# Block-sparse attention with a feed-forward layer: the first six tiles' scores as one product per block, neighbouring keys copied beside the sampled ones

## The chip, the cores and the metric

The kernel runs on one core of a Trainium2 chip. TensorE (PE in the profile), VectorE (DVE), ScalarE (ACT) and GpSimd (POOL) each work through their own instruction stream in order; SyncE (SP) issues most of the transfers, POOL and ACT some. The metric is the device time of one execution in microseconds, lower is better. Before the change three runs gave 733.46, 733.47 and 734.31 us, a median of 733.47 us.

## The reference

Four batches of 768 tokens, 8 heads of 64 numbers, blocks of 32 tokens (24 blocks per batch). The attention is masked by blocks, and its output goes through a feed-forward layer with a squared ReLU:

```python
scores = scale * np.matmul(q, k.transpose(0, 1, 3, 2))
mask = np.abs(blk_i - blk_j) <= window            # window = 1: the neighbouring blocks
mask = mask | (blk_i == 0) | (blk_j == 0) | (blk_i == n_blocks - 1) | (blk_j == n_blocks - 1)
mask[qb's rows, kb's columns] = True              # three sampled blocks per query block
attn = softmax(where(mask, scores, -1e9));  x = attn @ v
h = np.maximum(x @ w_in, 0.0)                     # 3072 x 512 by 512 x 2048
return h * h @ w_out                              # 3072 x 2048 by 2048 x 512
```

So a query block (other than the first and the last) sees 8 blocks of keys: two fixed ones (first and last), three sampled, three neighbouring. The first and the last query block see everything. All is float32.

## The kernel before

**Tiles.** A tile is 128 tokens of a batch, four query blocks; a batch has six tiles, and three tiles make a chunk, the unit of the feed-forward layer. There are 24 tiles and 8 chunks. A `Half` is one tile with four of the eight heads; a `Whole` is the first and the last query block of a batch with one pair of heads. Below, H10 is the half of tile 1 with heads 0 to 3, H11 that with heads 4 to 7, and W0 to W3 are the four wholes of batch 0.

**Stages.** The head (to about 50 us) does W0, W1, H00, W2, W3, H01, H10, H11, H20, H21 in this order, five steps of a hand-written clock (`now`) apart. Then comes chunk 0 of the feed-forward layer, and beside it the halves of tiles 3 to 5; later chunks run beside later tiles. A half goes through fixed steps: scores (PE, into PSUM), maxima (DVE), exponentials (ACT), turn (PE transposes into PSUM), copies (out of PSUM into `pT`, one of 512 numbers per partition for each of `e` = 0 and 1), values (PE, line 532), norm (DVE, lines 548 to 563). The classes yield how many steps of the clock to wait; within an engine the instructions run in the order in which this loop emits them, so an instruction that waits holds up all behind it on its engine.

**Keys.** `KN` holds all keys of the batch, by block. `KG` holds per query block up to 8 slots: two fixed, three sampled, three neighbouring. From tile 6 on (`MOVED`) the slots are loaded by DMA (`load_kg`), and the scores are one product of 256 columns per block and head (line 408). For the first six tiles POOL copies fixed (line 308) and sampled blocks (line 278) from `KN` into `KG`, and the scores take two products: 96 columns of neighbours straight from `KN` and 160 columns from `KG` (both line 426).

**Values.** `V[k][0]` has the two fixed blocks and two sampled ones for each query block of tile k, `V[k][1]` the third sampled one and three neighbours. Sampled blocks come by DMA on SP (`load_sampled`, line 334), nine or twelve transfers per tile. The fixed ones of tile 0's first query block come by DMA and are copied by ACT to the other places (`copy_static`, line 218). Neighbours of tile 0 come by DMA (`load_window`, line 320); those of tiles 1 and 2 are copied from `vn`, all values of the batch (`copy_window`, line 226): 36 copies on POOL, 12 on ACT.

**Weights.** `cut_load` (POOL, line 801) fetches a raw block, `cut` (ACT, lines 817 and 819) and `cut_bits` (DVE, lines 828 and 829) turn it into float32. In chunk 0 each block is then split into two parts by ACT (line 861) and POOL (line 864; lines 835 and 836 for the first one).

Of the kernel before, what the change touches and what calls it, by code (L numbers as in the profile page):

```python
# [10 lines left out]
F32 = mybir.dt.float32  # L11
# [11 lines left out]
B, H, S, D = 4, 8, 768, 64  # L23
BLK = 32
NBLK = S // BLK
NRAND = 3
P = 128
NT = S // P
NJ = P // BLK
NPAIR = H // 2  # L30
# [44 lines left out]
CUT_0 = (35, 5)  # L75
CUT_1 = 3

MOVES_0 = 22


FIXED_0 = 7
FIRST_LOADS, SECOND_LOADS, THIRD_LOADS = 2, 3, 4
LATE = (0, 4)
KEYS_N = 2
MOVED = 6
# [1 line left out]


WO_LOW = 3
PLAIN = 16  # L90


# [5 lines left out]
def tile_block_sparse_attention_moe(ctx: ExitStack, tc, kd, knd, qd, qgd, vd, vnd, samp, wcat, out):  # L98
# [60 lines left out]
    QG = one.tile([P, NPAIR, 2, BLK], F32, name="QG")  # L159
    KN = one.tile([P, 2, NBLK, 2, BLK], F32, name="KN")  # L160
    V = {0: [one.tile([P, NJ, 2, HW // 2], F32, name=f"V{c}") for c in range(2)]}
    W1 = {f: one.tile([P, DM], F32, name=f"W1{f}") for f in range(1, NF)}
    KG = [one.tile([P, NJ, NSLOT // BLK, NPAIR, BLK], F32, name=f"KG{i}") for i in range(2)]
    WO = {f: one.tile([P, DM], F32, name=f"WO{f}") for f in range(WO_LOW)}

# [68 lines left out]
    def groups(t):  # L234

        return (2, 3, 1) if t == 0 else tuple(range(NJ - 1 if t == NT - 1 else NJ))

    def centre(qb):
        return min(max(qb, 1), NBLK - 2)
# [12 lines left out]
    def load_q(b, t, eng=nc.sync, own=None):  # L252
        q = (own or rot).tile([P, NJ, NPAIR, BLK], F32, tag="q", name=f"q{b}_{t}", bufs=1 if own else 2)
        n = NJ * NPAIR * BLK
        eng.dma_start(q.rearrange("p a b c -> p (a b c)"), qd[b, :, t * n : (t + 1) * n])
        st["q", b, t] = q

    def keys_of(b, t, own):

        k = order.index((b, t))  # L260
        st["kg", b, t] = (
            own.tile([P, NJ, 2 + NRAND, NPAIR, BLK], F32, name=f"KG{k}") if own else KG[(k - (k >= UC)) % 2]
        )
        return st["kg", b, t]

    def copy_keys(b, t, own=None):

        vals = sampled(t, 0, POOL)
        kg = keys_of(b, t, own)
        for us in (slice(0, 1), slice(1, 2)) if t == 0 else (slice(0, 2),):  # L270
            if t < UC:
                for u in range(us.start, us.stop):
                    static_keys(b, t, u, nc.gpsimd.tensor_copy)
            for j in sorted(groups(t)):
                for r in range(NRAND):
                    to = kg[:, j, 2 + r].rearrange("p (u i) s -> p u (i s)", u=2)
                    of = KN.rearrange("p u k i s -> p u k (i s)")
                    nc.gpsimd.tensor_copy(to[:, us].unsqueeze(2), of[:, us, bass.ds(vals[NRAND * j + r], 1)])  # L278
                yield
# [3 lines left out]

    def load_kg(b, t):
        vals = sampled(t, 0, SP)
        kg = keys_of(b, t, None)
        k4 = kd[b].rearrange("p (a c) -> p a c", a=NBLK)
        for j in sorted(groups(t)):
            for r in range(NRAND):
                nc.sync.dma_start(  # L290
                    kg[:, j, 2 + r].rearrange("p b c -> p (b c)").unsqueeze(1), k4[:, bass.ds(vals[NRAND * j + r], 1), :]
                )
        if t < 2:
            for i in range(2):
                src = k4[:, i * (NBLK - 1)].unsqueeze(1)
                dst = kg[:, :, i].rearrange("p j b c -> p j (b c)")
                nc.sync.dma_start(dst, src.broadcast_to(list(dst.shape)))
        js = sorted(groups(t))
        src = k4[:, NJ * t + js[0] - 1]
        n = src.shape[-1]  # L300
        src = bass.AP(src.tensor, src.offset, [src.ap[0], [n, len(js)], [1, 3 * n]])
        nc.sync.dma_start(kg[:, js[0] : js[0] + len(js), 2 + NRAND :].rearrange("p j w b c -> p j (w b c)"), src)

    def static_keys(b, t, u, copy):

        src = st["kn", b, u][:, 0 : NBLK : NBLK - 1].rearrange("p i a c -> p i (a c)").unsqueeze(1)
        dst = st["kg", b, t][:, :, 0:2, 2 * u : 2 * u + 2].rearrange("p j i a c -> p j i (a c)")
        copy(dst, src.broadcast_to(list(dst.shape)))

    def load_window(k, u, eng=nc.sync):  # L310
        us = halves(k, u)
# [48 lines left out]
    class Half:  # L360
# [37 lines left out]

        def scores(self):
            b, t, u = self.b, self.t, self.u  # L400
            q, kg, kn = st["q", b, t], st["kg", b, t], st["kn", b, u]
            self.sb = [bank(f"s{self.name}_{e}") for e in range(2)]
            for i in range(2) if self.moved else ():
                pr = 2 * u + i
                for g, j in enumerate(self.js):
                    for e in range(2):
                        r = slice(e * D, (e + 1) * D)
                        nc.tensor.matmul(  # L408
                            self.sb[e][g * BLK : (g + 1) * BLK, i * NSLOT : (i + 1) * NSLOT],
                            q[r, j, pr, :],  # L410
                            kg[r, j, :, pr, :],
                            start=True,
                            stop=True,
                        )
            for i in range(2) if not self.moved else ():
                pr = 2 * u + i
                for piece in range(2):
                    for g, j in enumerate(self.js):
                        c = centre(NJ * t + j)
                        for e in range(2):  # L420
                            r = slice(e * D, (e + 1) * D)
                            if piece == 0:
                                k, a, z = kn[r, c - 1 : c + 2, i, :], S_WIN, NSLOT
                            else:
                                k, a, z = kg[r, j, : 2 + NRAND, pr, :], 0, S_WIN
                            nc.tensor.matmul(  # L426
                                self.sb[e][g * BLK : (g + 1) * BLK, i * NSLOT + a : i * NSLOT + z],
                                q[r, j, pr, :],
                                k,
                                start=True,  # L430
                                stop=True,
                            )

        def maxima(self):
            m = self.m = rot.tile([P, 2, 2], F32, tag="m", name=f"m{self.name}", bufs=4)
# [59 lines left out]
        def copies(self, pt):  # L495
            self.pT = rot.tile([P, NJ, 4, 2, BLK], F32, tag="pT", name=f"pT{self.name}", bufs=2)
            n = len(self.js)
            for e in range(2):
                src = pt[e].rearrange("p (h j q) -> p h j q", h=4, j=NJ)[:, :, :n]
                dst = self.pT[:, :n, 2 * e : 2 * e + 2].rearrange("p j i c q -> p (i c) j q")  # L500
                if e == 0 or self.k < UC:
                    nc.scalar.copy(dst, src)
                else:
                    nc.vector.tensor_copy(dst, src)
# [340 lines left out]
    def cut_next():  # L845

        nonlocal done
        n = len(cuts)
        for stage, lag in ((cut, AHEAD), (cut_bits, AHEAD + 1), (cut_split, AHEAD + 2), (cut_load, 0)):
            if 0 <= done - lag < n:  # L850
                stage(*cuts[done - lag])
        done += 1
# [150 lines left out]
    for k in range(1, UC):  # L1003
# [4 lines left out]
    load_keys(0, 1, nc.gpsimd)  # L1008
    load_sampled(0, 0, nc.sync, SP)
    load_q(0, 1)  # L1010
    load_sampled(1, 0, nc.sync, SP)
    load_q(0, 2, own=begin)
    load_sampled(2, 1, nc.sync, SP)
    windows = {
        (k, u): [(copy_window, k, u, j, n) for j in range(NJ) for n in range(3)]
        for k in range(1, UC)
        for u in range(2)
    }
    first = copy_keys(0, 0)
    for _ in groups(0):  # L1020
        next(first)
# [3 lines left out]
    for _ in range(EARLY_CUTS):  # L1025
        cut_next()
    deque(copy_keys(0, 1), 0)
    for i in range(AHEAD + 1):
        if i == FIRST_LOADS:
            for f, *at in windows[1, 0]:  # L1030
                f(*at, nc.gpsimd.tensor_copy)
        if i == SECOND_LOADS:
            deque(copy_keys(0, 2, begin), 0)
        if i == THIRD_LOADS:
            for f, *at in windows[2, 0] + windows[2, 1]:
                f(*at, nc.gpsimd.tensor_copy)
        if EARLY_CUTS <= i < AHEAD:
            cut_next()
    fixed = [(copy_static, k, i) for k in range(UC) for i in range(2)]
    moves = windows[1, 1]  # L1040
    side = lambda name: ps_o.tile([P, 512], F32, tag="o", name=name)
    work = Stream()
    for at, u in units(0):
# [2 lines left out]
    while work.todo or work.running:  # L1046
        work.step(now)
        now += 1
        if now % KEYS_N == 0 and later and next(later[0], True):
            later.pop(0)  # L1050
        if now >= FIXED_0 and fixed:
            f, *at = fixed.pop(0)
            f(*at, nc.scalar.copy)
        if now >= MOVES_0 and moves:
            f, *at = moves.pop(0)
            f(*at, nc.scalar.copy)
        if now >= CUT_0[0] and (now - CUT_0[0]) % CUT_0[1] == 0:
            cut_next()
    start.__exit__(None, None, None)
# [85 lines left out]
```

## Time and profile before

| | |
|---|---|
| median of the runs | 733.47 us |
| time of the profiled execution | 733.34 us |
| its span, first to last instruction | 731.6 us |
| PE busy | 707.5 us (97%) |
| DVE, ACT, POOL busy | 513.6, 507.2, 502.5 us (69 to 70%) |
| granted TensorE clock | 0.999 |
| moved by DMA | 108.42 MB |

In a row of the timeline the columns are the start in us, the duration, engine, source line, operation, output and input tiles with their shapes, the count, and in brackets the idle time of the engine ahead of it and what ended it. Rows of the groups give count, busy us and mean ns of one, then the idle time ahead of them. SPq and ACTq are instructions that issue transfers. PE is at 97% over the whole span, but at 5, 7 and 8 tenths in the first slices of 18.3 us: the head is where PE has room.

### The profile page before, as it was taken

How to read it: one execution, taken by the hardware profiler on the slowest of the kernel's cores; microseconds unless marked ns; L12 is line 12 of the kernel's file. 1: busy time of each engine (PE TensorE's matmuls, PEld its weight loads, DVE VectorE, ACT ScalarE, POOL GpSimd, SP SyncE). 2: the span in 40 equal slices, each digit the busy share in tenths (PEclk: the TensorE clock that was granted, in tenths of full speed). 3: DMA queues.
4: the chain of work that ended last, by engine and by line, in shares of the span. 5: the costliest groups of instructions: out<-in, count | busy, mean ns of one | idle time of the engine just before them, and what ended most of it. 6: DMA issues, size and time to landing. Idle time of an engine off the chain costs nothing.

```text
span 731.6 us, 22308 instructions
## 1 busy us (share of the span) xinstructions
PE 707.5 (97%) x8000; PEld 577.6 (79%) x8000; DVE 513.6 (70%) x1018; ACT 507.2 (69%) x1122; POOL 502.5 (69%) x606
## 2 busy tenths in 40 slices
PE   5789999999999999999999999999999999999997
PEld 3676775677888888877888888887888888889896
DVE  5876665868787867668886876768887676645442
ACT  5977777988876875588877776578877777533222
POOL 5994444347876676768878577666877577768884
PEclk9999999999999999999999999999999999999999
DMA  9958899746445547656455457665555351101001
GB/s 278 271 144 262 248 272 337 207 114 202 130 112 141 167 99 221 190 126 176 125 131 145 126 146 218 173 144 173 134 138 146 97 164 45 35 1 44 1 1 43
DMA packets 99232, 108.42 MB, mean 148 GB/s; under 512 B 13985, under 2 KB 85666, under 8 KB 99122
## 3 DMA queue, kind: packets, MB, share of 16 engines
q1 hardware_dynamic: 92866, 83.42, 42.7%
q0 software_dynamic: 5680, 22.27, 9.3%
q8 instruction: 64, 1.05, 0.6%
q10 hardware_dynamic: 576, 1.31, 0.5%
q14 instruction: 46, 0.38, 0.2%
HBM read 100.65 MB, written 6.29 MB: 146 GB/s over the span
## 4 chain that ended last, share of the span: by engine, by line
PE 80%; ACT 6%; DVE 5%; POOL 4%; issue 2%; DMA 1%; POOLq 1%; ACTq 0%; DVEq 0%
PE ph L901 34%; PE po L941 32%; PE s L408 5%; PE pv L517 5%; POOL V L226 2%; PE po L930 2%; POOL KG L278 2%; PE pv L702 1%; ACT craw L819 1%; DMA V<-in_v_dram 1%; PE g L636 1%; ACT p L477 1%; DVE WO L828 1%; DVE WO L829 1%; ACT wi L861 1%
## 5 line engine op out<-in xcount | busy, mean ns | idle before, releaser
L463 ACT ACTIVATE pm<-p 32x256 f32<-32x256 f32 x528 | 219.3, 415 | 24.6 <-DVE p L446 16.6
L864 POOL TENSOR_TENSOR wi<-W,wi 128x512 fp32r<-128x512 f32 x120 | 156.3, 1303 | 69.0 <-ACT wi L861 30.1
L901 PE MATMUL ph<-xh,wi 128*128 128x384 f32 x960 | 201.1, 347 | 2.0 <-DVE wi L863 1.6
L901 PEld LDWEIGHTS ph<-xh,wi 128*128 128x128 f32 x960 | 170.2, 188 | 25.8 <-issue 11.0
L864 POOL TENSOR_TENSOR wo<-WO,wo 128x512 fp32r<-128x512 f32 x112 | 145.1, 1295 | 51.7 <-DVE wo L863 50.9
L941 PE MATMUL po<-wo,gh 128*128 128x512 f32 x672 | 175.3, 396 | 0.0
L905 ACT ACTIVATE r<-ph 128x384 f32<-128x384 f32 x128 | 62.7, 490 | 151.3 <-PE ph L901 150.9
L920 POOL TENSOR_TENSOR gl<-gf,gh 128x384 fp32r<-128x384 f32 x112 | 113.8, 1016 | 71.9 <-DVE gf L917 59.6
L917 DVE SCALAR_TENSOR_TENSOR gf<-ph,r 128x384 f32<-128x384 f32 x112 | 61.9, 552 | 124.0 <-ACT r L905 124.0
L941 PEld LDWEIGHTS po<-wo,gh 128*128 128x128 f32 x672 | 124.0, 188 | 25.9 <-issue 4.5
L901 PE MATMUL ph<-xl,wi 128*128 128x384 f32 x480 | 103.9, 338 | 0.0
L941 PE MATMUL po<-wo,gl 128*128 128x512 f32 x336 | 98.6, 402 | 0.0
L901 PEld LDWEIGHTS ph<-xl,wi 128*128 128x128 f32 x480 | 85.4, 188 | 0.1
L941 PEld LDWEIGHTS po<-wo,gl 128*128 128x128 f32 x336 | 62.1, 189 | 21.5 <-issue 4.3
L863 DVE TENSOR_REDUCE wo<-WO 128x512 fp32r<-128x512 f32 x112 | 74.9, 669 | 0.0
L863 DVE TENSOR_REDUCE wi<-W 128x512 fp32r<-128x512 f32 x105 | 70.5, 672 | 0.0
L438 DVE TENSOR_REDUCE m<-s 128x2 f32<-128x512 f32 (+1 forms) x96 | 61.7, 684 | 7.3 <-PE s L426 3.5
L912 ACT ACTIVATE gh<-r 128x384 fp32r<-128x384 f32 x112 | 58.9, 526 | 9.5 <-POOL wo L864 0.4
L446 DVE TENSOR_TENSOR p<-s,m 128x512 f32<-128x512 f32 (+1 forms) x72 | 46.1, 681 | 0.3
L930 PE MATMUL po<-WO,gp 128*128 128x512 f32 x96 | 44.8, 601 | 0.0
L469 DVE STREAM_TRANSPOSE pT<-pm 128x1024 f32<-128x1024 f32 (+1 forms) x36 | 41.3, 1146 | 0.3 <-ACT pm L463 0.3
L408 PE MATMUL s<-KG,q 64*32 64x256 f32 x1056 | 39.8, 382 | 1.4 <-ACT p L477 1.4
(102 smaller groups left out, 755.5 us busy)
## 6 DMA issues: line engine op xcount, KB each, us to landing
craw<-in_w_dram POOLq DMA_DIRECT2D x32, 512.0 KB, 5.4
V<-in_v_dram SPq DMA_DIRECT2D x462, 32.5 KB, 2.3
KG<-in_k_dram SPq DMA_DIRECT2D x198, 64.0 KB, 2.0
V<-in_v_dram SPq DMA_DIRECT2D x28, 390.0 KB, 6.1
KG<-in_k_dram SPq DMA_DIRECT2D x12, 768.0 KB, 6.4
q<-in_q_dram SPq DMA_DIRECT2D x24, 256.0 KB, 3.1
out_dram<-ot SPq DMA_DIRECT2D x22, 256.0 KB, 5.3
V<-in_v_dram SPq DMA_DIRECT2D x14, 292.5 KB, 5.3
```

Of the source, the lines that this page charges most:

```text
L408: nc.tensor.matmul(self.sb[e][g * BLK : (g + 1) * BLK, i * NSLOT : (i + 1) * NSLOT], q[r, j, pr, :], kg[r, j, :, pr, :], start=True, stop= ...
L438: nc.vector.tensor_reduce(m[at, e], self.sb[e][at].rearrange("p (i c) -> p i c", i=2), axis=AX, op=ALU.max)
L463: nc.scalar.activation(p[a * BLK : (a + 1) * BLK, g], x[g * BLK : (g + 1) * BLK, :, a], AF.Exp, scale=SCALE)
L863: nc.vector.tensor_reduce(w[:, 0], src.unsqueeze(2), axis=AX, op=ALU.max)
L864: nc.gpsimd.tensor_tensor(w[:, 1], src, w[:, 0], op=ALU.subtract)
L901: nc.tensor.matmul(ph[:, :TOK], w, x, start=(i == 0), stop=(i == len(steps) - 1))
L905: nc.scalar.activation(r, ph[:, :TOK], AF.Relu)
L912: nc.scalar.activation(gh, r, AF.Square)
L917: nc.vector.scalar_tensor_tensor(gf, ph[:, :TOK], 0.0, r, op0=ALU.max, op1=ALU.mult)
L920: nc.gpsimd.tensor_tensor(gl, gf, gh, op=ALU.subtract)
L930: nc.tensor.matmul(acc[c][u], g[:, u * P : (u + 1) * P], WO[f], start=(f == 0), stop=(f == NF - 1))
L941: nc.tensor.matmul(acc[c][u], g[:, at], w[:, k], start=first, stop=(f == NF - 1 and g is gl))
```

## The change

- Scores of tiles 0 to 5: one product of 256 columns, as in the later tiles. `window_keys` copies the three neighbours into `KG` with one POOL copy per tile and half of the heads (128 partitions, 4 x 3 x 64 numbers; three query blocks in tile 0 and tile 5), between the fixed and the sampled copies.
- The neighbours of tiles 1 and 2 in `V` come by DMA on SP, one `load_window` each, ahead of the sampled blocks of the same tile. The 48 `copy_window` are gone.
- The fixed blocks of tiles 1 and 2 in `V` are copied by POOL (four copies of 64 partitions, 4 x 260 numbers) instead of ACT; those of tile 0 stay on ACT.
- The `e` = 1 copy of the halves of tiles 0 to 2 goes from ACT to DVE, as it already was for tiles 3 to 5.
- The third set of slots (`KG2`), now of 8 slots, shares memory with the weight blocks 8 to 15 of `W1`, which become one tile `W1B`.

```diff
-    W1 = {f: one.tile([P, DM], F32, name=f"W1{f}") for f in range(1, NF)}
+    W1 = {f: one.tile([P, DM], F32, name=f"W1{f}") for f in range(1, W1_LATE)}
+    W1B = one.tile([P, NF - W1_LATE, DM], F32, name="W1B")
+    W1.update({f: W1B[:, f - W1_LATE] for f in range(W1_LATE, NF)})
+    KG2 = W1B.rearrange(...)
...
     def copy_keys(b, t, window=nc.gpsimd.tensor_copy):
...
+            for u in range(us.start, us.stop):
+                window_keys(b, t, u, window)
...
+    def window_keys(b, t, u, copy):
+        js = sorted(groups(t))
+        first = NJ * t + js[0] - 1
+        kn = st["kn", b, u][:, first]
+        src = bass.AP(kn.tensor, kn.offset, [kn.ap[0], [2 * BLK, len(js)], [2 * BLK, 3], [1, 2 * BLK]])
+        dst = st["kg", b, t][:, js[0] : js[0] + len(js), 2 + NRAND :, 2 * u : 2 * u + 2]
+        copy(dst.rearrange("p j w a c -> p j w (a c)"), src)
...
-            for i in range(2) if self.moved else ():
+            for i in range(2):
...
-                if e == 0 or self.k < UC:
+                if e == 0:
                     nc.scalar.copy(dst, src)
                 else:
                     nc.vector.tensor_copy(dst, src)
...
     load_q(0, 1)
+    load_window(1, 0)
     load_sampled(1, 0, nc.sync, SP)
     load_q(0, 2, own=begin)
+    load_window(2, 1)
     load_sampled(2, 1, nc.sync, SP)
...
-    for i in range(AHEAD + 1):
-        if i == FIRST_LOADS:
-            for f, *at in windows[1, 0]:
-                f(*at, nc.gpsimd.tensor_copy)
-        if i == SECOND_LOADS:
-            deque(copy_keys(0, 2, begin), 0)
-        if i == THIRD_LOADS:
-            for f, *at in windows[2, 0] + windows[2, 1]:
-                f(*at, nc.gpsimd.tensor_copy)
-        if EARLY_CUTS <= i < AHEAD:
-            cut_next()
-    fixed = [(copy_static, k, i) for k in range(UC) for i in range(2)]
-    moves = windows[1, 1]
+    for i in range(2):
+        copy_static(1, i, nc.gpsimd.tensor_copy)
+    cut_next()
+    deque(copy_keys(0, 2), 0)
+    for i in range(2):
+        copy_static(2, i, nc.gpsimd.tensor_copy)
+    for _ in range(EARLY_CUTS + 1, AHEAD):
+        cut_next()
+    fixed = [(FIXED_0[k] + i, k, i) for k in range(1) for i in range(2)]
```

More of the change, by code (lines that the diff above doesn't have):

```diff
@@ L76 @@
 CUT_1 = 3
-MOVES_0 = 22
-FIXED_0 = 7
-FIRST_LOADS, SECOND_LOADS, THIRD_LOADS = 2, 3, 4
+FIXED_0 = (7, 14, 24)
 LATE = (0, 4)
@@ L89 @@
 WO_LOW = 3
+W1_LATE = NF - NJ * NSLOT * NPAIR // DM
 PLAIN = 16
@@ L161, in tile_block_sparse_attention_moe @@
     V = {0: [one.tile([P, NJ, 2, HW // 2], F32, name=f"V{c}") for c in range(2)]}
-    W1 = {f: one.tile([P, DM], F32, name=f"W1{f}") for f in range(1, NF)}
+    W1 = {f: one.tile([P, DM], F32, name=f"W1{f}") for f in range(1, W1_LATE)}
+    W1B = one.tile([P, NF - W1_LATE, DM], F32, name="W1B")
+    W1.update({f: W1B[:, f - W1_LATE] for f in range(W1_LATE, NF)})
+    KG2 = W1B.rearrange("p f (a c s) -> p f a c s", c=NPAIR, s=BLK).rearrange("p (j i) a c s -> p j (i a) c s", j=NJ)
     KG = [one.tile([P, NJ, NSLOT // BLK, NPAIR, BLK], F32, name=f"KG{i}") for i in range(2)]
@@ L256, in load_q, with keys_of, copy_keys @@
         st["q", b, t] = q
-    def keys_of(b, t, own):
+    def keys_of(b, t):
         k = order.index((b, t))
-        st["kg", b, t] = (
-            own.tile([P, NJ, 2 + NRAND, NPAIR, BLK], F32, name=f"KG{k}") if own else KG[(k - (k >= UC)) % 2]
-        )
+        st["kg", b, t] = KG2 if k == UC - 1 else KG[(k - (k >= UC)) % 2]
         return st["kg", b, t]
-    def copy_keys(b, t, own=None):
+    def copy_keys(b, t, window=nc.gpsimd.tensor_copy):
         vals = sampled(t, 0, POOL)
-        kg = keys_of(b, t, own)
+        kg = keys_of(b, t)
         for us in (slice(0, 1), slice(1, 2)) if t == 0 else (slice(0, 2),):
@@ L285, in load_kg @@
         vals = sampled(t, 0, SP)
-        kg = keys_of(b, t, None)
+        kg = keys_of(b, t)
         k4 = kd[b].rearrange("p (a c) -> p a c", a=NBLK)
@@ L400, in scores @@
             b, t, u = self.b, self.t, self.u
-            q, kg, kn = st["q", b, t], st["kg", b, t], st["kn", b, u]
+            q, kg = st["q", b, t], st["kg", b, t]
             self.sb = [bank(f"s{self.name}_{e}") for e in range(2)]
-            for i in range(2) if self.moved else ():
+            for i in range(2):
                 pr = 2 * u + i
@@ L414, in scores @@
                         )
[L415 to L432, printed above, removed]
         def maxima(self):
@@ L1010, in tile_block_sparse_attention_moe @@
     load_q(0, 1)
+    load_window(1, 0)
     load_sampled(1, 0, nc.sync, SP)
     load_q(0, 2, own=begin)
+    load_window(2, 1)
     load_sampled(2, 1, nc.sync, SP)
[L1014 to L1018, printed above, removed]
     first = copy_keys(0, 0)
@@ L1050, in tile_block_sparse_attention_moe @@
             later.pop(0)
[L1051 to L1056, printed above, removed]
+        if fixed and now >= fixed[0][0]:
+            copy_static(*fixed.pop(0)[1:], nc.scalar.copy)
         if now >= CUT_0[0] and (now - CUT_0[0]) % CUT_0[1] == 0:
```

## The prediction

> **What bounds the kernel now.** First the page: the span, the busy shares and the slices.
>
> ```profile
> span 731.6 us, 22308 instructions
> PE 707.5 (97%) x8000; PEld 577.6 (79%) x8000; DVE 513.6 (70%) x1018; ACT 507.2 (69%) x1122; POOL 502.5 (69%) x606
> PE   5789999999999999999999999999999999999997
> q8 instruction: 64, 1.05, 0.6%
> ```
>
> PE idles 24.1 us in all, most of it in the first slices, the head. The edit works in the head and in chunk 0. Second, busy time of the stages: columns are the stretch, its length, then busy us (and instructions) of PE, PEld, DVE, ACT, POOL, the granted clock, DMA share and GB/s.
>
> ```profile
> 13.40:32.10 18.70, 14.96 (x405) 11.21 (x408) 17.54 (x53) 18.14 (x41) 17.91 (x56) 1.00 0.96 263
> 32.10:50.60 18.50, 14.49 (x470) 11.81 (x461) 14.13 (x32) 16.90 (x35) 17.57 (x46) 1.00 0.65 182
> ```
>
> In the head three engines are nearly full: from 13.4 to 32.1 DVE, ACT and POOL each work 17.5 to 18.1 of 18.7 us. So taking work from ACT and POOL helps only as far as DVE, which gets more, allows. Third, what DVE waits for between 13.4 and 50, with the two instructions at the ends of its chain.
>
> ```profile
> 13.45 1.28 DVE L438 TENSOR_REDUCE m<-s 96x2 f32<-96x512 f32 x2 [1.35 <-PE s L426]
> 48.79 0.42 DVE L563 TENSOR_TENSOR x<-pv,rec 128x256 f32<-128x256 f32 x1
> DVE m L438 <- PE s L426: 2.2, 2, 1.4
> DVE rec L548 <- PE pv L532: 2.1, 4, 0.8
> DVE W L828 <- ACT craw L819: 0.4, 1, 0.4
> ```
>
> From H00's maxima (13.45) to the norm that ends H21 (48.79 + 0.42 = 49.21) DVE needs 35.76 us. Of these it waits 0.9 (the 2.2 less the 1.35 ahead of 13.45) + 2.1 + 0.4 = **3.4 us**. That is all that the head can give while DVE's own work stays.
>
> **Part 1: copies from ACT to DVE.** The `e` = 1 copies of six halves, two of 384 numbers (tile 0) and four of 512. DVE has done such copies; what counts is how much later the next instruction starts.
>
> ```profile
> 23.11 0.56 DVE L690 COPY pTg<-ptg 128x384 f32<-128x384 f32 x1
> 23.58 1.27 DVE L438 TENSOR_REDUCE m<-s 96x2 f32<-96x512 f32 x2
> 67.36 0.68 DVE L504 COPY pT<-pt 128x512 f32<-128x512 f32 x1
> 67.96 1.28 DVE L438 TENSOR_REDUCE m<-s 128x2 f32<-128x512 f32 x2
> ```
>
> 23.58 - 23.11 = 0.47 and 67.96 - 67.36 = 0.60, so DVE gains 2 x 0.47 + 4 x 0.60 = **3.34 us** in the very stretch where it has 3.4 us of waits. The end of the head can come 0.06 us earlier if every wait closes, and 3.34 us later if none does.
>
> Which close? ACT loses these copies and more (below), so exponentials and the other half of `pT` are there earlier, and three of the four waits for values, the one for scores and the one for `craw` can close. The last one, before H21's norm, can't: H21's values start when DVE has copied; DVE has a pair of weight steps of 1.5 us to do meanwhile, and the values take 1.1 us, or 1.8 us with a stall as below. I leave 0.3 us. Part 1: -0.06 + 0.3 = **+0.24**, bounds -0.06 and +3.34.
>
> **Part 2: less on ACT and POOL.**
>
> ```profile
> L226 POOL COPY V<-vn 32x260 f32<-32x260 f32 x36 | 16.0, 443 | 1.6
> L278 POOL COPY KG<-KN 128x64 f32 x18 | 3.3, 234 | 0.0
> L308 POOL COPY KG<-KN 128x512 f32<-128x512 f32 x6 | 3.5, 613 | 6.4 <-DMA KN<-in_kn_dram 6.4
> L226 ACT COPY V<-vn 32x260 f32<-32x260 f32 x12 | 4.9, 406 | 0.3 <-DMA vn<-in_vn_dram 0.2
> L218 ACT COPY V<-V 64x1040 f32<-64x1040 f32 x4 | 4.0, 1066 | 0.0
> L502 ACT COPY pT<-pt 128x512 f32<-128x512 f32 x12 | 6.6, 588 | 1.4 <-PE pt L492 1.3
> ```
>
> ACT loses 4.9 + 4.0 + (4 x 0.59 + 2 x 0.47, the second an estimate by the 384-number copy of part 1) = 12.2 us of its 35. It stops being a bound; nothing on it is late next. POOL: by its two rows a copy costs (613 - 234) / 448 = 0.85 ns more per number, so 576 numbers cost 0.67, 768 cost 0.83, 1040 cost 1.06 us (estimates). It loses 16.0 and gets 2 x 0.67 + 8 x 0.83 (tiles 0 to 4) + 4 x 1.06 = 12.2, so 3.8 us less before chunk 0. In its queue tile 1's slots fill 0.67 + 2 x 0.83 = 2.3 us later (tile 0's first window fits into the 3.42 us for which POOL waits for `KN`, below), tile 2's 0.67 + 4 x 0.83 + 2 x 1.06 - 12 x 0.44 = 0.8 later; their scores start 5.4 and 4.0 us after the slots are full now, which hides it. Tile 5's two copies fall into chunk 0, where POOL has gaps. Worth **0** on the path: POOL and ACT ran beside DVE. Were that cover gone, the scores, and DVE behind them, would be late by the whole 2.3 and 0.8; bounds 0 and +2.3.
>
> **Part 3: scores.**
>
> ```profile
> 62.70 0.40 PE L426 MATMUL s<-KN,q 64*32 64x96 f32 x16
> 63.84 2.84 PE L930 MATMUL po<-WO,gp 128*128 128x512 f32 x6
> 161.42 1.09 PE L408 MATMUL s<-KG,q 64*32 64x256 f32 x32
> 162.45 0.98 PE L901 MATMUL ph<-xh,wi 128*128 128x384 f32 x4
> ```
>
> A half's scores cost 63.84 - 62.70 = 1.14 us in two products and 162.45 - 161.42 = 1.03 in one: half the instructions save a tenth, since the columns that stream are the same. In the head PE is not the bound. In chunk 0 the first half's 0.11 us (H30, 51.5 us) lies ahead of the first `r`, for which ACT waits; after that the chain of waits runs ACT and DVE in turn, the matmuls wait for the exponentials ahead of each transpose, and a faster product gains nothing. **-0.11**, bounds 0 and -0.5 (four times 0.11, twice 0.03 for tile 5).
>
> What may count more is PE's own program:
>
> ```profile
> 31.74 1.11 PE L532 MATMUL pv<-V,pT 128*32 128x65 f32 x48 [1.49 <-ACT p L477]
> 36.50 1.07 PE L532 MATMUL pv<-V,pT 128*32 128x65 f32 x58 [1.25 <-DMA q<-in_q_dram]
> 40.45 0.46 PE L426 MATMUL s<-KG,q 64*32 64x160 f32 x4 [0.75 <-issue]
> 43.36 1.78 PE L532 MATMUL pv<-V,pT 128*32 128x65 f32 x64 [0.38 <-ACT pT L502]
> ```
>
> PE stops in the middle of a group of like matmuls, where its operands have long been there, every 126 or so matmuls (58 + 8 + 60 from 36.50 to 40.45). The queue q8 brought 64 packets for 16,000 PE instructions, 250 each, which fits: I read these stops as waits for instructions. The head issues 176 matmul records fewer, so one stop of 0.7 to 1.5 us goes and the others move (by my count to H11's scores and the values of H10, H11 and H21). Only the last lies on the path; it is in the 0.3 us above.
>
> **Part 4: transfers.** Two windows of 780 KB go ahead of tile 1's and tile 2's sampled blocks on SP.
>
> ```profile
> 14.31 0.58 POOL L231 DMA_DIRECT2D vn<-in_vn_dram  x1
> 20.84 1.24 ACT L226 COPY V<-vn 32x260 f32<-32x260 f32 x3 [0.18 <-DMA vn<-in_vn_dram]
> 23.72 0.91 PE L702 MATMUL pvg<-vn,pTg 128*64 128x65 f32 x22 [0.58 <-DVE pTg L690]
> ```
>
> SP issues two transfers more, under 0.5 us each; behind them stand sampled blocks and q tiles that are wanted 5 us and more after they land now. The 1.6 MB are 6.1 us of all engines at the stretch's 263 GB/s. The first wanted behind them is `vn` of W2 and W3: issued 0.67 later, at 15.0, it lands at 21.5 if it still takes 20.84 - 14.31 = 6.5 us, and W2's values want it at 23.72 + 0.47. **0**, with 2.7 us to spare; bounds 0 and, if all 6.1 us came ahead of it, +3.4.
>
> **Part 5: DVE against POOL.**
>
> ```profile
> 54.06 1.30 POOL L864 TENSOR_TENSOR wi<-W,wi 128x512 fp32r<-128x512 f32 x1
> 54.13 1.80 DVE L828 SCALAR_TENSOR_TENSOR WO<-WO,craw 128x512 int32<-128x512 int32 x1
> 55.96 0.69 DVE L829 SCALAR_TENSOR_TENSOR WO<-craw,WO 128x512 int32<-128x512 int32 x1
> L443 DVE TENSOR_SCALAR m<-m 128x4 f32<-128x4 f32 x4 | 1.3, 316 | 0.1
> 54.05 0.17 DVE L443 TENSOR_SCALAR m<-m 128x4 f32<-128x4 f32 x1
> L828 DVE SCALAR_TENSOR_TENSOR W<-W,craw 128x512 int32<-128x512 int32 x3 | 2.3, 759 | 0.4 <-ACT craw L819 0.4
> ```
>
> L828 took 1.80 us beside a POOL instruction of 1.30 and normally takes 0.69; in the head L443 takes 0.32 instead of 0.17 and the weight steps 0.76. So DVE loses some 6 x 0.146 + 8 x 0.07 = 1.4 us there to POOL. POOL's copies become longer (0.83 to 1.06 instead of 0.44) until about 40 us and rarer after it. I take **-0.3**, for the last three weight pairs without POOL beside them; bounds -1.4 and +2.0 (both losses grown 2.4 times with the copies' length). By the Trainium skill ("SBUF — State Buffer", Who interferes with whom) a VectorE instruction with two SBUF inputs is held for the whole length of a GpSimd instruction that reads SBUF; the 1.80 agrees, and by that rule alone the sum would stand at the +2.0.
>
> **Sum:** +0.24 + 0 - 0.11 + 0 - 0.3 = -0.17, so 733.34 - 0.17 = 733.17, say **733.2 us** (the profiled execution is 0.13 under the median, the three runs spread 0.85).
>
> **The rivals.**
> *Faster, DVE is let go:* all waits close (-0.06), the 1.4 us of collisions vanish, and one such lock in chunk 0's chain (about 1.0 us) goes too: -0.06 - 1.4 - 1.0 - 0.11 = -2.6, **730.8**. For it: POOL has 3.8 us less, ACT 12. Against: POOL stays full to about 40 us.
> *Slower, longer POOL copies hold DVE:* in the head, where L443 and the weight steps meet copies of 0.83 to 1.06 us: +2.0 instead of -0.3, **735.5**. It decides as soon as L443's mean passes 0.5 us. For it: the 1.80 row. Against: not every DVE instruction meets a long copy.
> *Slower, the windows crowd the start:* `vn` lands after 24.2 and W2's values, then DVE, wait; with half of the 6.1 us ahead of it +0.4, with all +3.4, about **735.1**. Against: it is in another queue than the windows.
> *The shared tile makes weights wait:* if a write into one block of `W1B` waited for readers of another, 8 blocks by the 1.3 us of L864 cost up to 10 us, **743**. Against it:
>
> ```profile
> 5.91 0.60 POOL L308 COPY KG<-KN 128x512 f32<-128x512 f32 x1 [2.96 <-DMA KN<-in_kn_dram]
> 12.17 0.61 POOL L308 COPY KG<-KN 128x512 f32<-128x512 f32 x1 [3.42 <-DMA KN<-in_kn_dram]
> ```
>
> POOL copied from the first half of `KN` at 5.91 while the second was on its way until 12.17, so parts of a tile are kept apart.
>
> **Numbers.** Forecast 0.44, faster rival 0.29, long copies 0.13, windows 0.11, shared tile 0.03. A change under 0.2% (1.5 us) can't be told from none. The forecast gives 0.36 to same and 0.04 to either side, the faster rival 0.27 to faster, the slower ones 0.21 to slower, the rest to same: faster 0.31, same 0.44, slower 0.25. Range 730.4 to 735.8; the forecast's own is 732.0 to 734.6.
>
> **What would show it.** Right: DVE without waits from 13.4 to 48, the last norm of H21 ending at 48.7 to 49.7, ACT with some 12 us idle in the head, the first hidden product at 50 to 51, four stops of PE instead of five. Wrong: that product before 49, which means DVE's instructions became shorter; or after 52, with L443 over 0.5 us or a wait for `vn` as its sign; or ACT's line 817 waiting for line 864 in chunk 0.

## The result and the profile after

The changed kernel takes **744.73 us** (median, 741.74 to 746.21), the kernel before on the same chip 733.73 us: a ratio of 1.0144, 95% interval 1.0109 to 1.0179, so 8 to 13 us slower. The forecast was 733.2 us with a range up to 735.8: wrong in sign and size. The profiled execution of after took 743.68 us, 10.3 more than that of before.

Of the page of after its span and the instruction queue; then two stretches that the prediction showed for before, and the one from 20 to 30 us (length, busy us of PE, PEld, DVE, ACT, POOL, granted clock, DMA share, GB/s):

```profile
span 741.9 us, 21574 instructions
...
q8 instruction: 61, 1.00, 0.6%
```

```profile
13.40:32.10 18.70, 7.79 (x130) 5.38 (x136) 18.21 (x27) 3.95 (x9) 18.70 (x48) 0.76 1.05 288
32.10:50.60 18.50, 16.28 (x411) 11.13 (x407) 17.68 (x47) 13.49 (x29) 10.60 (x32) 0.97 0.87 243
20.00:30.00 10.00, 0.98 (x28) 0.98 (x30) 9.82 (x11) 1.05 (x2) 10.00 (x28) 0.66 1.02 320
```

DVE is busy 18.21 of 18.70 us, yet finishes 27 instructions there where before it finished 53. From 20 to 30 us PE works 0.98 us and ACT 1.05, where in before they worked 9.03 and 9.54: both wait for DVE. PE's granted clock, 1.00 there in before, sinks to 0.66 while it idles. What DVE does in that time stands in its timeline, and beside it that of POOL:

```profile
16.76 1.38 DVE L643 TENSOR_TENSOR mo<-mg,negative 64x2 f32<-64x2 f32 x2
18.17 8.74 DVE L644 SCALAR_TENSOR_TENSOR mg<-mg,mo 128x2 f32<-128x2 f32 x1
```

```profile
16.18 1.18 POOL L308 COPY KG<-KN 128x512 f32<-128x512 f32 x2
17.29 1.59 POOL L317 COPY KG<-KN 128x768 f32<-128x768 f32 x2
18.83 2.89 POOL L278 COPY KG<-KN 128x128 f32 x12
21.67 2.04 POOL L218 COPY V<-V 64x1040 f32<-64x1040 f32 x2
23.66 0.53 POOL L792 DMA_DIRECT2D craw<-in_w_dram  x1
24.19 1.17 POOL L308 COPY W1B<-KN 128x512 f32<-128x512 f32 x2
25.30 1.59 POOL L317 COPY W1B<-KN 128x768 f32<-128x768 f32 x2
26.84 2.90 POOL L278 COPY W1B<-KN 128x128 f32 x12
```

An instruction on 128 x 2 numbers takes **8.74 us** (line 644, the scaled maximum of a whole; line 653 in before). All that time POOL works on without a pause. I call this a hold. PE and the end of the head follow from it:

```profile
29.02 1.52 PE L523 MATMUL pv<-V,pT 128*32 128x65 f32 x36 [10.29 <-DVE pT L495]
...
62.17 0.96 PE L892 MATMUL ph<-xh,WI 128*128 128x384 f32 x4 [0.78 <-ACT xh L881]
```

In before that first hidden product stood at

```profile
50.60 0.97 PE L901 MATMUL ph<-xh,WI 128*128 128x384 f32 x4 [0.82 <-ACT xh L890]
```

The groups of DVE's small instructions, of after (11 to 62 us) and then of before (11 to 52 us), by line and shape: count, busy us, mean ns.

```profile
L644 DVE SCALAR_TENSOR_TENSOR mg<-mg,mo 128x2 f32<-128x2 f32 x2 | 8.9, 4452 | 0.1
L643 DVE TENSOR_TENSOR mo<-mg,negative 64x2 f32<-64x2 f32 x4 | 3.3, 833 | 0.1
L434 DVE TENSOR_SCALAR m<-m 128x4 f32<-128x4 f32 x4 | 1.6, 404 | 0.1
L434 DVE TENSOR_SCALAR m<-m 96x4 f32<-96x4 f32 x2 | 0.4, 186 | 0.1
```

```profile
L443 DVE TENSOR_SCALAR m<-m 128x4 f32<-128x4 f32 x4 | 1.3, 316 | 0.1
L652 DVE TENSOR_TENSOR mo<-mg,negative 64x2 f32<-64x2 f32 x4 | 0.9, 219 | 0.1
L443 DVE TENSOR_SCALAR m<-m 96x4 f32<-96x4 f32 x2 | 0.6, 284 | 0.1
L653 DVE SCALAR_TENSOR_TENSOR mg<-mg,mo 128x2 f32<-128x2 f32 x2 | 0.4, 182 | 0.1
```

These four kinds of instruction took 14.2 us instead of 3.2, 11.0 more; the first hidden product starts 62.17 - 50.60 = 11.6 us later. Chunk 0 makes good about 1 us. The loss lies in the head and, by this reading, in the holds. About 1 us of it comes by way of the clock, which is 0.83 from 50 to 60 us: PE's eight transposes at 54.99 take 1.97 us there, those at 45.15 take 1.09, and DVE waits 1.07 us for them.

The second reading is the transfers, in the list of issues from 10 to 45 us (median us from issue to landing), of before and then of after:

```profile
craw<-in_w_dram POOLq DMA_DIRECT2D x5, 512.0 KB, 4.5
V<-in_v_dram SPq DMA_DIRECT2D x26, 65.0 KB, 4.7
vn<-in_vn_dram POOLq DMA_DIRECT2D x1, 780.0 KB, 6.5
```

```profile
craw<-in_w_dram POOLq DMA_DIRECT2D x7, 512.0 KB, 7.9
V<-in_v_dram SPq DMA_DIRECT2D x25, 65.0 KB, 7.2
...
vn<-in_vn_dram POOLq DMA_DIRECT2D x1, 780.0 KB, 9.5
```

These three kinds take 2.5 to 3.4 us longer; the q tiles in the same list hardly do (4.9 us before, 5.1 after). In after, `vn` is hidden behind the hold; without it, it need not be.

### The profile page after: what moved, and what is told of

Same layout as the page of the kernel before. It is cut to its first block, busy times and chain, and to the rows that moved or that the text cites. A ratio compares the mean times of both kernels' runs of the same rounds, so it can differ in the third digit from the quotient of the medians.

```text
span 741.9 us, 21574 instructions
## 1 busy us (share of the span) xinstructions
PE 708.6 (96%) x7648; PEld 574.1 (77%) x7648; DVE 526.7 (71%) x1024; ACT 496.2 (67%) x1100; POOL 499.5 (67%) x586
## 4 chain that ended last, share of the span: by engine, by line
PE 84%; DVE 7%; DMA 4%; ACT 3%; issue 1%; ACTq 0%; SPq 0%; DVEq 0%
PE ph L892 34%; PE po L932 31%; PE s L417 6%; PE pv L508 5%; PE po L921 3%; DMA V<-in_v_dram 3%; PE pv L693 1%; PE g L627 1%; DVE mg L644 1%; PE pv L523 1%; DVE m L429 1%; PE pt L483 1%; ACT p L468 1%; DMA QG<-in_qg_dram 1%; DVE mg L640 1%
## 5 line engine op out<-in xcount | busy, mean ns | idle before, releaser
L892 PEld LDWEIGHTS ph<-xh,wi 128*128 128x128 f32 x960 | 170.2, 188 | 24.5 <-issue 11.6
L855 POOL TENSOR_TENSOR wi<-W,wi 128x512 fp32r<-128x512 f32 x56 | 73.0, 1303 | 46.2 <-DVE wi L854 18.2
L855 POOL TENSOR_TENSOR wi<-W1B,wi 128x512 fp32r<-128x512 f32 x64 | 83.9, 1312 | 27.4 <-ACT wi L852 24.8
L429 DVE TENSOR_REDUCE m<-s 128x2 f32<-128x512 f32 (+1 forms) x96 | 61.7, 684 | 6.7 <-PE s L417 6.3
L417 PE MATMUL s<-KG,q 64*32 64x256 f32 x1344 | 51.4, 386 | 1.5 <-ACT p L468 1.5
```

Source lines behind the costliest of these rows:

```text
L417: nc.tensor.matmul(self.sb[e][g * BLK : (g + 1) * BLK, i * NSLOT : (i + 1) * NSLOT], q[r, j, pr, :], kg[r, j, :, pr, :], start=True, stop= ...
L429: nc.vector.tensor_reduce(m[at, e], self.sb[e][at].rearrange("p (i c) -> p i c", i=2), axis=AX, op=ALU.max)
L855: nc.gpsimd.tensor_tensor(w[:, 1], src, w[:, 0], op=ALU.subtract)
L892: nc.tensor.matmul(ph[:, :TOK], w, x, start=(i == 0), stop=(i == len(steps) - 1))
```

## The experiments

The theories: **holds** (DVE's small instructions that read and write SBUF are held by POOL's run of copies), **transfers** (the two windows crowd the DMA engines, so `vn` and PE's instructions come late) and **copies** (the `e` = 1 copies given to DVE). "After" and "before" below are the two kernels; each ratio is against before on the same chip, with its 95% interval.

### Maxima of the wholes kept in PSUM

```diff
-            m = self.m = rot.tile([P, 2], F32, tag="mg", ...)
+            self.m = rot.tile([P, 2], F32, tag="mg", ...)
+            m = self.sg[0][:, 508:510]
...
-            nc.vector.scalar_tensor_tensor(m, m, -SCALE, other, ...)
+            nc.vector.scalar_tensor_tensor(self.m, m, -SCALE, other, ...)
```

> The changed kernel, but the wholes' maxima go into a PSUM column and only the last step of them into SBUF, so that line 643's and line 644's counterparts on DVE have one SBUF input each instead of two. Theory A (a DVE instruction with two SBUF inputs can't start while POOL's copies follow each other without a gap; this made W2's line 644 last 8.74 us): the step takes 0.2 us, the head ends 8 to 9 us earlier, 744.7 - 8.6 = 736, between 734.5 and 738. Theory B (the two added transfers crowd the first 30 us, the long instruction is only where it shows) and theory C (the copies that went to DVE): no change, 743 to 746.

Measured 740.47 us, ratio 1.0074 (1.0051 to 1.0097). DVE's timeline, then POOL's:

```profile
21.01 0.33 DVE L644 TENSOR_TENSOR mo<-g,negative 64x2 f32<-64x2 f32 x2
21.38 0.16 DVE L645 SCALAR_TENSOR_TENSOR mg<-g,mo 128x2 f32<-128x2 f32 x1
...
23.20 1.27 DVE L429 TENSOR_REDUCE m<-s 96x2 f32<-96x512 f32 x2
24.51 3.99 DVE L434 TENSOR_SCALAR m<-m 96x4 f32<-96x4 f32 x1
```

```profile
23.26 2.04 POOL L218 COPY V<-V 64x1040 f32<-64x1040 f32 x2
...
26.88 1.59 POOL L317 COPY W1B<-KN 128x768 f32<-128x768 f32 x2
28.42 0.75 POOL L278 COPY W1B<-KN 128x128 f32 x3
```

The same computation with one input in PSUM takes 0.33 and 0.16 us beside the same copies. But the next DVE instruction with only SBUF operands, the halves' scaling on 96 x 4 numbers, is now held for 3.99 us. So the hold moved, and only part of the time came back.

### Pauses between POOL's copies

```diff
+                nc.gpsimd.memset(rest, 0.0)      # 64 numbers, after each fixed, window and static copy, and each three sampled
```

> The changed kernel with a POOL instruction that reads no SBUF (a memset of 64 numbers) after each fixed copy, each window copy and each group of three sampled copies. Theory A: DVE gets in at the first pause, so no hold is longer than 1.7 us (a group); 744.7 - 7 = 737.5, between 735 and 740, though POOL has some 3 us more work. Theories B and C: no gain, 744 to 747.

Measured 740.5 us, ratio 1.0093 (1.006 to 1.0125). The longest hold is 1.75 us:

```profile
32.60 1.75 DVE L439 TENSOR_SCALAR m<-m 128x4 f32<-128x4 f32 x1
```

Pauses break the long hold and leave many of 0.8 to 1.75 us.

### Less on POOL, and the copies given back to ACT

The fixed `v` copies of tiles 1 and 2 on ACT:

> The changed kernel with the fixed v copies of tiles 1 and 2 on ACT again (four copies of 1.04 us away from POOL). Theory A: POOL's chain without a gap is 2.0 us shorter between W2's maxima and its end, so the hold is 8.7 - 2.0 - 0.5 = 6 us or less: 739 to 742.5, less still if the chain now breaks at the transfer that POOL issues. Theory B: 743 to 746. Theory C: 743 to 746.

Measured 741.72 us, ratio 1.0114 (1.0082 to 1.0146); the hold at line 644 shrinks to 2.85 us, others of 1 to 2 us stay. With the `e` = 1 copies of the first six halves back on ACT instead (`if e == 0 or self.k < UC`):

> The changed kernel with the e = 1 copies of tiles 0 to 2 on ACT again. Theory C: 744.7 - 3.3 = 741.4 or less, with the long step gone or short. Theory A: the step in question comes before the first of these copies, so it still lasts 8 to 9 us; DVE has 3.3 us less to do after it, ACT 3.3 more: 741.5 to 745. Theory B: 743 to 746.

Measured 742.89 us, ratio 1.0102 (1.0078 to 1.0127), and DVE's timeline:

```profile
19.47 8.72 DVE L644 SCALAR_TENSOR_TENSOR mg<-mg,mo 128x2 f32<-128x2 f32 x1
```

The hold is as long without these copies, and a second one, at line 643, takes 4.86 us where after had 1.98, so this run does not price the copies by themselves. Its interval and that of after overlap. The copies theory isn't needed: the last kernel of the table below keeps these copies on DVE and loses nothing.

### Each half of the change alone

First the scores alone: one product, window copies on POOL and the shared tile, all the rest as before.

> One product for the first six tiles alone: the window copies on POOL and the third set of slots in W1B as in the change, but the v windows copied by POOL and ACT, the fixed v copies and the e = 1 copies on ACT as before. POOL has 8 us more to do in the head than before the change. Theory A: the window copies (0.8 us, back to back) hold DVE, 2 to 6 us, and POOL's longer queue makes tile 2's slots late: 736 to 744. Without theory A only the queue counts: 734 to 737.

Measured 740.93 us, ratio 1.0096 (1.0079 to 1.0113). Here the 36 copies of line 226 are still in POOL's queue between the key copies; holds are shorter (line 644 takes 3.3 us in three instructions, 2.86 of it in one), but POOL has too much, and PE waits 2.23 us for `WI` from it.

Then the transfers alone: before, with the two `load_window` on SP in place of the 48 copies.

> The kernel before with one part of the change alone: the neighbouring v blocks of tiles 1 and 2 by transfer, where the change has them; the 48 copies of them on POOL and ACT are gone, all else is as before. Theory B: vn lands late and W2's values wait 2 to 4 us, so 735 to 738. Without theory B: POOL loses 16 us, ACT 5, DVE has the same work and fewer holds: 732 to 734. Theory A says nothing against a gain here, as POOL gets no copy that it didn't have.

Measured 740.58 us, ratio 1.0095 (1.0072 to 1.0117). PE's rows at the places where the prediction found stops of 1.49 and 1.25 us:

```profile
35.32 1.11 PE L532 MATMUL pv<-V,pT 128*32 128x65 f32 x48 [2.01 <-issue]
...
43.37 1.91 PE L532 MATMUL pv<-V,pT 128*32 128x65 f32 x58 [4.54 <-issue]
```

The same matmuls of the same program now wait 2.01 and 4.54 us, and no engine releases them. That fits the reading of these stops as waits for PE's own instructions, and the DMA packets of the two traces bear it out. The packets of the instruction queue q8 that matter here end at 30.33 and 35.11 us in before and at 33.93 and 41.97 here; PE goes on 1.4 us after each (31.74 and 36.50; 35.32 and 43.37). The last one takes hardly longer than its counterpart (1.23 us, 1.05 in before), but it starts later. So before with the transfers takes about 7 us more (0.95%), with 20 us of work taken off POOL and ACT. Not all of this need be the transfers': with the copies gone from POOL's queue, line 652's two instructions for W3, 0.50 us in before, take 2.75.

To tell the transfers from the removal of the copies: before with all its copies, and two transfers of the same size into memory nobody reads.

```diff
+    def spare_window(k):
+        src = vd[0, (NJ * k - 1) * BLK : (NJ * k + 1 + NJ) * BLK]
+        src = bass.AP(src.tensor, src.offset, [[HW, 3 * BLK], [BLK * HW, NJ], [1, DM]])
+        nc.sync.dma_start(W1B[BLK:P, NJ * (k - 1) : NJ * k], src)
...
+    spare_window(1)
     load_sampled(1, 0, nc.sync, SP)
     load_q(0, 2, own=begin)
+    spare_window(2)
     load_sampled(2, 1, nc.sync, SP)
```

> The kernel before with all its copies, and two more transfers of a window's size (96 partitions x 4 x 512 numbers each) at the same two places in SP's queue, into memory that nobody reads. Transfers: their volume delays the values' blocks and PE's instruction packets, 738 to 741 us, PE's stops of 1.49 and 1.25 us grown to 2 us and more. If the loss of the run with windows alone came from the removal of the 48 copies or from the windows' own readers: 733.5 to 735.

Measured 742.59 us, ratio 1.0104 (1.0075 to 1.0132). `vn` takes 10.9 us to land instead of 6.5, ACT's copies from it wait 4.78 us, and PE behind them:

```profile
vn<-in_vn_dram POOLq DMA_DIRECT2D x1, 780.0 KB, 10.9
```

```profile
27.28 1.32 PE L704 MATMUL pvg<-vn,pTg 128*64 128x65 f32 x24 [4.35 <-ACT pTg L692]
...
47.84 0.46 PE L428 MATMUL s<-KG,q 64*32 64x160 f32 x4 [1.78 <-issue]
```

Volume alone does it; it is bytes that nobody waits for, and the hold of the last run is no part of it (the two instructions for W3 take 0.57 us). The stops grew less here than was expected (1.78 at the scores), the wait for `vn` more.

### Holds and transfers, with and without each other

After, with the maxima in PSUM as above, and the scaling of the halves' maxima on ACT in the first three tiles, so that of the kinds of instruction that can be held only the weight steps are left on DVE there:

```diff
-                nc.vector.tensor_scalar(m[at], m[at], -SCALE, None, op0=ALU.mult)
+                if self.k >= UC:
+                    nc.vector.tensor_scalar(m[at], m[at], -SCALE, None, op0=ALU.mult)
...
+            if self.k < UC:
+                nc.scalar.mul(self.m[at], self.m[at], -SCALE)
```

> The changed kernel with the wholes' maxima in a PSUM column (as in the first experiment) and the scaling of the halves' maxima (line 434's counterpart, from SBUF to SBUF on DVE) done by ACT just ahead of the exponentials, for tiles 0 to 2. No DVE instruction but the weight steps can then be held by POOL's copies in the head. Theory A (the holds cost about 11 us in the changed kernel's profile): the head is shorter by that, as far as the values of W2 don't wait for vn: 744.7 - 11 + 2 = 736, between 734 and 738. Theory B (the two transfers make vn late by 4 us and more): W2's values start only at about 26 us, so not under 735.5.

> The same, and the two window transfers moved back on SP: tile 1's behind tile 1's sampled blocks and the q tile, tile 2's behind tile 2's sampled blocks. Theory B: vn lands 3 to 4 us earlier than with the windows in front and the head ends 2 to 3 us earlier: 733 to 735. Without theory B: as the kernel before it in this list, within 0.7 us.

Measured 737.2 us, ratio 1.0049 (1.0025 to 1.0072), and with the windows one place later in SP's queue (behind tile 1's and tile 2's sampled blocks) 737.59 us, ratio 1.0043 (1.0026 to 1.006). DVE's maxima keep their length beside POOL's copies; three of the weight steps, 0.7 us otherwise, take 1.2 to 1.5. A later place trades the wait for `vn` for a stop of PE of 2.40 us.

Now without the windows: the neighbours' blocks of tiles 1 and 2 hold a constant. First with the holds, then without them:

> The changed kernel without its two window transfers for the values of tiles 1 and 2: their neighbouring v blocks hold a constant that ACT writes at the very start, so the neighbours' values of these tiles are left out of the result. Holds (DVE held by POOL's copies) and transfers (the windows crowd the DMA engines) both: the transfers were worth 3 us (changed kernel without its holds) to 6.3 us (transfers alone in the kernel before), so 738.4 to 741.7 us, with the long hold at line 644 still there. If the holds alone make the loss: 744 and more, as the changed kernel. If the transfers alone make it and the holds only fill time that is lost anyway: 734 to 735.

> As the run without windows (the neighbours' values of tiles 1 and 2 are left out), and besides the maxima of the wholes kept in PSUM and the scaling of the halves' maxima done by ACT in the first three tiles. If holds and transfers are all of the loss: 732.5 to 735.5 us, the first hidden product at 49 to 52 us. If a third cause is left (the copies moved to DVE, longer products, the shared tile): 736 or more.

And the control, before with the same edits against holds:

> Control: the kernel before with the same two edits against holds (maxima of the wholes in PSUM, scaling on ACT in the first three tiles). Holds: before has only some 1.4 us of them, so 732 to 734.5 us. If the edits make any kernel faster, whatever POOL copies: about 7 us less, 726 to 728.

| | with the two transfers | without them |
|---|---|---|
| small instructions of DVE held | 744.73 us, 1.0144 (1.0109 to 1.0179) | 742.52 us, 1.0108 (1.0082 to 1.0134) |
| not held | 737.2 us, 1.0049 (1.0025 to 1.0072) | **732.87 us**, 0.9971 (0.9953 to 0.9988) |

The control: 735.0 us, ratio 1.002 (0.9997 to 1.0043); the edits make no kernel faster by themselves. Three of its ten executions took 739.7 to 740.6 us; the profiled one is among them, and two weight steps, which the edits leave on DVE, took 3.03 and 2.69 us in it beside copies of line 278. So long holds can come with the queue of before too, in some executions. In the run without windows `L644` still takes 8.72 us, and `vn` lands after 6.2; without windows and holds:

```profile
vn<-in_vn_dram POOLq DMA_DIRECT2D x1, 780.0 KB, 6.3
```

```profile
13.40:32.10 18.70, 16.56 (x354) 11.44 (x348) 17.11 (x51) 10.00 (x27) 18.70 (x49) 1.00 0.90 254
```

DVE finishes 51 instructions again and the clock is 1.00. By the differences of the ratios, the holds cost 0.95% with the transfers and 1.37% without (7.0 and 10.1 us of 734), the transfers 0.36% with the holds (the intervals overlap) and 0.78% without (2.6 and 5.7 us). I had expected 738.4 to 741.7 for the run without windows; 742.52 is above that. It may be that late data costs less while DVE is held, but the intervals are too wide to show it. With both gone the rest of the change is 0.1 to 0.5% faster than before, but that kernel leaves the neighbours' values out, and any way to bring them costs something.

### Short copies instead of long ones

POOL's window copies of tiles 0 to 2 in three pieces and its static ones in four (192 to 260 numbers), back to back:

> The changed kernel, POOL's window copies of tiles 0 to 2 cut into three pieces each (256 or 192 numbers) and its static v copies into four (260 numbers), back to back as before. If an unbroken run of POOL's copies holds DVE, however short each is: a hold of 5 us or more at line 652 (the scaled maximum) stays, 743 to 748 us (POOL has some 5 us more). If the length of each copy does it: no instruction of DVE is longer than it should be by more than 0.5 us, first hidden product at 53 to 57 us, 737 to 741 us.

Measured 742.45 us, ratio 1.0102 (1.0073 to 1.0131). DVE, then POOL:

```profile
22.48 5.23 DVE L651 TENSOR_TENSOR mo<-mg,negative 64x2 f32<-64x2 f32 x2
```

```profile
23.23 2.82 POOL L316 COPY V<-V 64x260 f32<-64x260 f32 x8
26.00 0.53 POOL L800 DMA_DIRECT2D craw<-in_w_dram  x1
26.52 1.17 POOL L308 COPY W1B<-KN 128x512 f32<-128x512 f32 x2
27.63 2.10 POOL L312 COPY W1B<-KN 128x256 f32<-128x256 f32 x6
```

Beside pieces of 0.35 us two instructions on 64 x 2 numbers still take 5.23 us, at line 651 rather than at 652. So the length of each copy is not what makes a hold long; the theory by length falls. The time, though, is half a microsecond below the 743 to 748 us that I gave the theory of an unbroken run, and the longest hold is shorter than in after.

### Fewer weight blocks loaded ahead

Whether the windows could have the place of something else: three weight blocks of 512 KB ahead instead of five (`AHEAD = 3`), in after without holds, and in before (where the loop that places the window copies keeps its six turns):

> The changed kernel with the maxima of the wholes in PSUM, the scaling on ACT in the first three tiles, and three weight blocks of 512 KB loaded ahead in place of five (1.0 MB less in the head). If the windows cost their time because they share the engines with blocks that aren't wanted yet: 733.5 to 735.5 us, against 737.2 with five. If their own place in SP's queue is what costs: 736.5 to 738. If the blocks are then late: ACT waits for craw, 738 or more.

> Control: the kernel before with three weight blocks loaded ahead in place of five. If its transfers are not on its path: 733 to 734.5 us. If its head is bound by them too: 730 to 732. If the blocks are late then: 735 or more.

Measured 742.0 us, ratio 1.0097 (1.0071 to 1.0122), and 746.78 us, ratio 1.0164 (1.0139 to 1.019). In before with three, blocks are then late in the head:

```profile
52.60 0.66 ACT L817 ACTIVATE W<-craw 128x512 f32<-128x512 f32 x1 [3.76 <-DMA craw<-in_w_dram]
53.92 0.69 DVE L828 SCALAR_TENSOR_TENSOR W<-W,craw 128x512 int32<-128x512 int32 x1 [4.66 <-ACT craw L819]
```

The longest stop of both kernels comes later. In after with three, the head loses little (the first hidden product starts at 53.73 us, with five at 52.77), but PE then stands for values of a later tile:

```profile
128.68 0.40 PE L526 MATMUL pv<-V,pT 128*32 128x65 f32 x2 [8.44 <-DMA V<-in_v_dram]
```

Before with three has the same stop at 132.60, 6.55 us long. That the blocks which were not loaded ahead crowd these values is my reading; no run tests it. Two blocks fewer cost before 12 us, so the blocks ahead are wanted. No version measured here that computes everything beats the kernel before.

## Why the prediction was wrong

- **Part 5, DVE against POOL, is the step that failed.** It took -0.3, with a bound of +2.0 got by letting each collision grow with the length of a copy. The measured growth is 11.0 us in the trace, and 7.0 to 10.1 us of time when it is taken away. The slower rival had the mechanism ("longer POOL copies hold DVE") and the wrong unit: a hold does not last one copy, but can run over a score of instructions. The row I leaned on, 1.80 beside 1.30, was one held by one. What I didn't weigh is what stood in POOL's queue before, by the timeline and the copies of line 226 (minimum, median and maximum ns):

```profile
19.99 5.28 POOL L226 COPY V<-vn 32x260 f32<-32x260 f32 x12
```

```profile
L226 POOL COPY V<-vn x36: 395/398/857, 20.0 to 42.1; 32x260 f32<-32x260 f32 x36
```

  They started 5.28 / 12 = 0.44 us apart and took 0.40, so there was a gap of 0.04 after each. The change takes them out, and what follows in POOL's queue starts before its forerunner ends (12 copies of 0.29 us in 2.89). That the gaps had kept the holds short is argued, not shown. For it: the run with the transfers alone takes these copies out and gives POOL none, and line 652's two instructions for W3 go from 0.50 to 2.75 us. The run with the scores alone says nothing on it: its hold of 2.86 us ended at 21.47, before the first of these copies (22.23).
- **The sign I named was on the wrong line.** Line 443's mean was to pass 0.5 us; it became 0.404, while the wholes' maxima, which I had not priced at all, took 8.74. The other sign, a first hidden product after 52, did show it (62.17).
- **Part 4, transfers at nothing, failed too.** `vn` was to land in 6.5 us after issue; it took 9.5 (2.7 us to spare in the plan, 3.0 lost). The bound of +3.4 held only the delay of `vn`; PE's own instructions, whose packets I had counted, were never put into that price, and in the run with the transfers alone the stops grew by 0.5 and 3.3 us. Measured, by the ratios: 2.6 to 5.7 us within the change, 7.0 alone and 7.6 as spare bytes. The rival with the windows (735.1) had the mechanism; it named the mark of 24.2 us for `vn`, and by the median landing `vn` was there at 24.1, behind a hold, while without holds the transfers still cost 5.7.
- **Part 1, copies on DVE:** +0.24 within bounds up to +3.34; giving them back changed nothing that can be told apart. **Part 2** had its sizes right: window copies of 768 numbers took 0.83 us, of 576 0.67, static ones 1.05, as estimated, and ACT idled as foretold. But its 0 on the path rested on "POOL and ACT ran beside DVE", and that was the same error as part 5's: POOL was in DVE's way.
- **Part 3:** a half's scores take 1.09 us in chunk 0 as estimated; q8 brought 61 packets for 15,296 PE instructions, again 250 each, and the reading of PE's stops as waits for instructions held (above). The stop that was to go can't be read, since PE waited for DVE.
- **The shared tile** (743 us, which by its number came nearest) was not the cause: with `W1B` in place and both causes away the kernel takes 732.87.
- **The sum without parts 4 and 5** stands 0.13 us above before (+0.24 - 0.11). The kernel with both causes away is 0.9 to 3.4 us below before by its interval, so this part of the sum was a little too high, as far as a kernel that leaves the neighbours out, and from which before's own short holds are gone too, can say.

## What to carry to other kernels

Before joining many small copies on GpSimd into few long ones, look in the trace for VectorE's small instructions that read and write only SBUF, and ask where GpSimd's queue still has gaps; price a hold by the length of the whole run, not of one instruction. Keep such VectorE operands in PSUM or give the instruction to ScalarE: here this was worth 7 to 10 us. Where the DMA engines' share is 0.96 in a stretch, price added bytes by what each other transfer there then needs, the matrix engine's own instructions among them, not by the queue that they are issued on.

## What the runs showed of the hardware that was not expected

- A hold runs across many POOL instructions: 8.74 us over some 20 copies and a DMA issue of 0.53 us. By the Trainium skill ("SBUF — State Buffer", Who interferes with whom) a VectorE instruction with two SBUF inputs contends with a GpSimd instruction that reads SBUF, `tensor_scalar` can contend when it enters a two-port mode, and `tensor_reduce` never does. The traces agree on the first: two inputs in SBUF 8.74 us, with one of them in PSUM 0.16. The scaling, a `tensor_scalar` on 96 x 4 numbers, took 3.99; its mode no trace shows. `L429`'s two reductions took 1.27 beside the same copies, but they read PSUM, so they don't test the last. The page has the other engine blocked for the whole instruction; the runs show blocking over many.
- What lets DVE in is open. The holds shown end 0.02 to 0.03 us after a POOL copy ends (26.91 against 26.89, 28.50 against 28.47, 27.71 against 27.69), that is where one copy gives way to the next, but up to a score of such changes went by first. In these three the next copy begins a new group; in the run with the fixed copies on ACT the hold of 2.85 us ended inside one, at 21.19. Nor is a lack of gaps enough for a long hold: in before the sampled copies stood as close, and the scaling beside them took 0.30 us:

```profile
26.89 2.88 POOL L278 COPY KG<-KN 128x128 f32 x12
```

```profile
28.56 0.30 DVE L443 TENSOR_SCALAR m<-m 128x4 f32<-128x4 f32 x1
```

- In the four stops compared above PE goes on 1.4 us after its instruction packet has landed, and one of them grew from 1.25 to 4.54 us beside 1.6 MB of added transfers (the packet started later; share of the DMA engines 0.85 to 1.04 around it). PE's granted clock fell to 0.66 in a stretch in which it had worked 10%.
